# VectorE exps in fp16 with a set sign bit and a two-term polynomial, in a fused attention and GEGLU kernel

## Chip, cores, metric

One core of one Trainium2 chip. The metric is device time in microseconds (us), median of several executions.

## The reference

A pre-LayerNorm transformer block on 2048 tokens of width 512, 32 heads of width 16, in bf16:

```python
def _A_ref(x, wqkv, wo):          # attention
    ...
    scores = jnp.einsum("bhqd,bhkd->bhqk", q, k) * (Dh ** -0.5)
    p = _softmax(scores, axis=-1)
    o = jnp.einsum("bhqk,bhkd->bhqd", p, v)
    ...
def _B_ref(x, w_gate, w_up, w_down):
    return (_gelu(x @ w_gate) * (x @ w_up)) @ w_down
h  = x + _A_ref(_layernorm(x), A_wqkv, A_wo)
h2 = h + _B_ref(_layernorm(h), B_w_gate, B_w_up, B_w_down)
```

The work that matters is the softmax: 32 x 2048 x 2048 exponentials, in 2048 tiles of 128x512.

## The kernel before

The kernel has two complete paths. The fast path computes the softmax without subtracting a maximum and ends with a check of its row sums. If the check fails, every engine waits for the fast path's end and then runs a second, safe path (the `mx_` tiles) that subtracts the maximum.

```python
h.reg_load(r, flag[0:1, 0:1])
with h.If_ne(r, 128):              # 128 = every partition passed
    for sem, v in fin:
        if v:
            h.wait_ge(sem, v)
    FP.run(name, h)                # the second path
```

The reciprocals of the row sums are kept in `LINV`, with 16 columns for each of 40 units (a unit is a chunk of queries times a group of heads). Chunks are of 512, 512, 512, 256 and 256 queries; a unit of 256 queries writes only half of its columns:

```python
CHUNKS = (512, 512, 512, 256, 256)
LINV = at("LINV", [128, NUNIT, 16], FP32)
# [...] at the start, on GpSimd:
e.memset(LINV[:], 1.0)
# [...] at the end of unit u, nb = (queries of the chunk) / 128, so 4 or 2:
li = LINV[:, u, 0:4 * nb]...
e.reciprocal(out=li, in_=o4[:, :, :, 16])
# [...] the check, over the whole table; n = NUNIT * 16 = 640:
LCHK[:, n]   = (probe == 65535)                    # does the conversion to uint16 saturate?
LCHK[:, 0:n] = min(max(LINV, 2.0 ** -22), 2.0 ** 16) == LINV
lmin = reduce_min(LCHK)                            # then summed over 128 partitions into flag
```

(The last block is shortened from the four VectorE calls of the source.)

ScalarE does most exps, in steps of three and two tiles. VectorE does some, in groups of up to four tiles, from the bits of the score: `dX` is the score in units of 1/1024 octave (an octave is a factor of two of the exp) converted to uint16; the exponent bits become one factor, a polynomial of the mantissa the other. Matmuls, exps and VectorE's groups are put in order when the program is built, by a list scheduler that works with a modelled duration for every operation (the number after the engine's name). Each engine then runs its list in that fixed order.

```python
t1, t2 = 0.16 + 0.133 * n, 0.16 + 0.267 * n        # modelled us for n tiles
E = (X >> 3) & 0x1f80          # tensor_scalar, t1: 2^octave as bf16 bits
X = X & 0x3ff | 0x3c00         # tensor_scalar, t1: mantissa M as fp16 bits
W = M * M                      # tensor_tensor, t2
W = W * EK + EB                # tensor_scalar, t1
W = W * M                      # tensor_tensor, t2
T = W * E                      # tensor_tensor, t2
# P.V adds the products of V with E and with T
```

## Time and profile before

Before: 949.21 us, median of 3 (947.68 to 950.33). The parts that matter:

| what | before |
|---|---|
| span of the profiled run | 947.0 us |
| ScalarE (ACT) busy | 874.4 us, 92% |
| VectorE (DVE) busy | 735.3 us, 78% |
| exp tiles on ScalarE / on VectorE | 1832 / 216 |
| VectorE groups | 64 |

The busy line of the page of the kernel before (engine, busy us, share of the span, instructions; PE is TensorE's matmuls, PEld its weight loads, POOL is GpSimd):

```profile
PE 833.2 (88%) x7100; PEld 276.3 (29%) x7224; DVE 735.3 (78%) x1138; ACT 874.4 (92%) x817; POOL 220.5 (23%) x268
```

Groups of instructions of the kernel before, split by shape: line, engine, operation, output and input, count, then busy us and mean ns of one, then idle time just before them and what ended it. First the exps, then the three tensor-by-tensor products and the three operations with constants of one full VectorE group.

```profile
L1221 ACT ACTIVATE PT<-pbank 128x1536 bf16<-128x1536 f32 x366 | 555.3, 1517 | 21.1 <-PE pbank L1215 20.5
L1221 ACT ACTIVATE PT<-pbank 128x1024 bf16<-128x1024 f32 x367 | 402.1, 1096 | 3.7 <-PE pbank L1215 3.7
...
L1547 DVE TENSOR_TENSOR dX<-dW,dE_56 128x2048 bf16<-128x2048 f16 x42 | 54.7, 1303 | 0.6
L1545 DVE TENSOR_TENSOR dW<-dW,dX 128x2048 f16<-128x2048 f16 x42 | 52.4, 1248 | 1.0
L1543 DVE TENSOR_TENSOR dW<-dX 128x2048 f16<-128x2048 f16 x42 | 52.2, 1242 | 0.7
...
L1542 DVE TENSOR_SCALAR dX<-dX 128x2048 uint16<-128x2048 uint16 x42 | 31.0, 738 | 0.6
L1540 DVE TENSOR_SCALAR dE_56<-dX 128x2048 uint16<-128x2048 uint16 x42 | 30.6, 729 | 0.4
L1544 DVE TENSOR_SCALAR dW<-dW 128x2048 f16<-128x2048 f16 x42 | 29.7, 708 | 0.2
```

The idle column of the exps is the first thing to read: 24.8 us in all before 733 exps. ScalarE is the bound. Steps overlap at their ends: the two groups sum to 957.4 us, but the page's merged busy time of all exps is 841.0 us. So the cost of a tile is not 1517/3 ns but 841.0 us over 1832 tiles: 0.459 us.

Two stretches of 50 us of the kernel before, the first with attention alone, the second with an FFN block in flight (columns: stretch and its length, then busy us and instruction count of PE, PEld, DVE, ACT, POOL, then granted clock, DMA share, GB/s):

```profile
150.00:200.00 50.00, 43.25 (x341) 12.53 (x343) 46.29 (x61) 49.40 (x45) 0.00 (x0) 1.00 0.23 82
...
500.00:550.00 50.00, 43.78 (x304) 13.03 (x310) 43.40 (x60) 48.31 (x47) 25.05 (x21) 1.00 0.00 1
```

In attention alone VectorE is at 46 of 50 us and ScalarE at 49. In the FFN stretch GpSimd (POOL) runs three of the GELU's steps, and ScalarE is idle for 1.7 of 50 us, against 0.6 in the first stretch. Its waits in the whole kernel before (who waited for whom: us in total, times, longest us):

```profile
ACT PT L1221 <- PE pbank L1215: 24.2, 35, 2.8
ACT w_sb L1726 <- POOL w_sb L1719: 12.4, 15, 1.8
```

The second line: the Tanh of the GELU waiting for GpSimd. Three lines: the reciprocals and the check of the kernel before (the first two are groups by shape, the third is from the timeline, start and length first).

```profile
L1621 DVE RECIPROCAL LINV<-pbank 128x16 f32<-128x16 f32 x24 | 6.1, 252 | 11.2 <-PE pbank L1218 11.0
L1621 DVE RECIPROCAL LINV<-pbank 128x8 f32<-128x8 f32 x16 | 3.2, 200 | 4.8 <-PE pbank L1218 4.8
```

### The profile page before, as it was taken

How to read it: one execution, taken by the hardware profiler on the slowest of the kernel's cores; microseconds unless marked ns; L12 is line 12 of the kernel's file. 1: busy time of each engine (PE TensorE's matmuls, PEld its weight loads, DVE VectorE, ACT ScalarE, POOL GpSimd, SP SyncE). 2: the span in 40 equal slices, each digit the busy share in tenths (PEclk: the TensorE clock that was granted, in tenths of full speed). 3: DMA queues.
4: the chain of work that ended last, by engine and by line, in shares of the span. 5: the costliest groups of instructions: out<-in, count | busy, mean ns of one | idle time of the engine just before them, and what ended most of it. 6: DMA issues, size and time to landing. Idle time of an engine off the chain costs nothing.

```text
span 947.0 us, 17699 instructions
## 1 busy us (share of the span) xinstructions
PE 833.2 (88%) x7100; PEld 276.3 (29%) x7224; DVE 735.3 (78%) x1138; ACT 874.4 (92%) x817; POOL 220.5 (23%) x268
## 2 busy tenths in 40 slices
PE   8999888888898889888888988998898788899887
PEld 3322222222232222222222222222233222333345
DVE  7558989998979768699979788889958687643753
ACT  5789999999999999999999998999999799999962
POOL 6400000000027570000014564000003354302440
PEclk9999999999999999999999999999999899999999
DMA  5000006000000000000000000000000000000000
GB/s 178 1 1 1 1 1 244 1 2 1 12 2 1 1 1 12 23 1 2 1 12 1 1 1 1 12 23 1 1 8 19 1 1 1 2 12 24 2 7 21
DMA packets 12331, 15.13 MB, mean 16 GB/s; under 512 B 1744, under 2 KB 11216, under 8 KB 12240
## 3 DMA queue, kind: packets, MB, share of 16 engines
q1 hardware_dynamic: 12240, 13.90, 4.5%
q8 instruction: 59, 0.97, 0.5%
q14 instruction: 32, 0.26, 0.1%
HBM read 11.80 MB, written 2.10 MB: 15 GB/s over the span
## 4 chain that ended last, share of the span: by engine, by line
ACT 33%; PE 32%; DVE 16%; issue 14%; POOL 5%; ACTq 0%; DVEq 0%; POOLq 0%
ACT PT L1221 32%; PE pbank L1215 15%; PE pbank L1214 11%; PE pbank L1801 4%; POOL w_sb L1717 2%; DVE dX L1527 2%; POOL w_sb L1719 2%; DVE dW L1543 2%; DVE dE_56 L1540 1%; DVE dX L1542 1%; DVE dX L1547 1%; DVE g_sb L1715 1%; ACT w_sb L1726 1%; POOL w_sb L1718 1%; DVE w_sb L1727 1%
## 5 line engine op out<-in xcount | busy, mean ns | idle before, releaser
L1221 ACT ACTIVATE PT<-pbank 128x1536 bf16<-128x1536 f32 (+1 forms) x733 | 841.0, 1306 | 24.8 <-PE pbank L1215 24.2
L1215 PE MATMUL pbank<-QT,KT 32*128 32x512 bf16 (+1 forms) x2560 | 287.1, 341 | 71.7 <-ACT PT L1221 57.5
L1215 PE MATMUL pbank<-PT,VA 128*17 128x512 bf16 (+1 forms) x2307 | 187.6, 340 | 3.2 <-issue 1.8
L1527 DVE TENSOR_SCALAR dX<-pbank 128x512 uint16<-128x512 f32 x216 | 146.8, 686 | 45.9 <-PE pbank L1215 45.0
L1215 PEld LDWEIGHTS pbank<-QT,KT 32*128 32x128 bf16 x2560 | 77.0, 91 | 319.3 <-ACT PT L1221 220.6
L1801 PE MATMUL pbank<-ones_bf,zero_bf 128*128 128x512 bf16 x388 | 135.2, 388 | 13.5 <-DVE OA L1613 11.0
L1678 POOL TENSOR_SCALAR rstd_102<-mv_101 128x1 f32<-128x1 f32 x16 | 4.3, 269 | 510.4 <-DVE mv_101 L1676 510.3
L1717 POOL TENSOR_TENSOR w_sb<-g_sb 128x512 f32<-128x512 f32 (+1 forms) x56 | 65.3, 1166 | 168.2 <-DVE g_sb L1715 168.2
L1215 PEld LDWEIGHTS pbank<-PT,VA 128*17 128x17 bf16 x2307 | 47.5, 87 | 110.6 <-issue 98.1
L1547 DVE TENSOR_TENSOR dX<-dW,dE_56 128x2048 bf16<-128x2048 f16 (+3 forms) x64 | 73.2, 1144 | 1.0
L1719 POOL TENSOR_TENSOR w_sb<-w_sb,g_sb 128x512 f32<-128x512 f32 (+1 forms) x56 | 71.3, 1273 | 4.7
L1545 DVE TENSOR_TENSOR dW<-dW,dX 128x2048 f16<-128x2048 f16 (+3 forms) x64 | 71.0, 1109 | 1.4
L1543 DVE TENSOR_TENSOR dW<-dX 128x2048 f16<-128x2048 f16 (+3 forms) x64 | 70.7, 1105 | 1.2
L1801 PEld LDWEIGHTS pbank<-ones_bf,zero_bf 128*128 128x128 bf16 x459 | 37.3, 97 | 78.3 <-issue 61.7
L1727 DVE SCALAR_TENSOR_TENSOR w_sb<-w_sb,g_sb 128x512 f32<-128x512 f32 (+1 forms) x56 | 44.1, 787 | 20.6 <-ACT w_sb L1726 20.2
L1214 PE MATMUL pbank<-wd_sb,GUT 128*128 128x512 bf16 x211 | 56.0, 381 | 1.5 <-issue 1.3
L1715 DVE COPY g_sb<-pbank 128x512 f32<-128x512 f32 (+1 forms) x56 | 34.7, 619 | 18.6 <-PE pbank L1214 18.5
L1753 DVE SCALAR_TENSOR_TENSOR GUT<-pbank,w_sb 128x512 bf16<-128x512 f32 (+1 forms) x56 | 34.6, 619 | 15.5 <-PE pbank L1214 15.2
L1726 ACT ACTIVATE w_sb<-w_sb 128x512 f32<-128x512 f32 (+1 forms) x56 | 34.1, 609 | 12.4 <-POOL w_sb L1719 12.4
L1718 POOL TENSOR_SCALAR w_sb<-w_sb 128x512 f32<-128x512 f32 (+1 forms) x56 | 43.6, 779 | 4.9
L1540 DVE TENSOR_SCALAR dE_56<-dX 128x2048 uint16<-128x2048 uint16 (+3 forms) x64 | 43.5, 680 | 0.6
L1542 DVE TENSOR_SCALAR dX<-dX 128x2048 uint16<-128x2048 uint16 (+3 forms) x64 | 42.9, 670 | 1.2
(126 smaller groups left out, 694.0 us busy)
## 6 DMA issues: line engine op xcount, KB each, us to landing
xres<-in_A_x_dram SPq DMA_DIRECT2D x16, 128.0 KB, 2.2
out_dram<-out_sb SPq DMA_DIRECT2D x16, 128.0 KB, 1.7
wg_sb<-in_B_w_gate_dram SPq DMA_DIRECT2D x1, 1792.0 KB, 7.1
wu_sb<-in_B_w_up_dram SPq DMA_DIRECT2D x1, 1792.0 KB, 11.2
wd_sb<-in_B_w_down_dram SPq DMA_DIRECT2D x1, 1792.0 KB, 17.0
x_sb<-in_A_x_dram SPq DMA_DIRECT2D x3, 512.0 KB, 8.3
wqkv_sb<-in_A_wqkv_dram SPq DMA_DIRECT2D x1, 896.0 KB, 7.5
x_sb<-in_A_x_dram SPq DMA_DIRECT2D x2, 256.0 KB, 2.9
```

Of the source, the lines that this page charges most:

```text
L1214: return lambda e: e.matmul(o, l, r, start=start, stop=stop)
L1215: return lambda e: e.matmul(o, l, r, start=start, stop=stop, tile_position=tile)
L1221: return lambda e: e.activation(out=o, in_=i, func=func, **kw)
L1527: yield Op("dve", 0.7, lambda e: e.tensor_scalar(out=dX[:, G["k"] % NX, j, :], in0=pbank[:, b, :], scalar1=1024.0 * CENTER, scalar2=0.0, o ...
L1543: yield Op("dve", t2, lambda e: e.tensor_tensor(out=W, in0=M, in1=M, op=ALU.mult), reads=kX, writes=kW)
L1545: yield Op("dve", t2, lambda e: e.tensor_tensor(out=W, in0=W, in1=M, op=ALU.mult), reads=kW + kX, writes=kW)
L1547: yield Op("dve", t2, lambda e: e.tensor_tensor(out=T, in0=W, in1=E, op=ALU.mult), reads=kW + kE, writes=kX)
L1717: yield Op("pool", 0.1 + 1.03 * nq / 512, lambda e: e.tensor_tensor(out=ws, in0=gs, in1=gs, op=ALU.mult), reads=[("g", i)], writes=[("w", i)])
L1718: yield Op("pool", 0.1 + 0.7 * nq / 512, lambda e: e.tensor_scalar(out=ws, in0=ws, scalar1=GA, scalar2=1.0, op0=ALU.mult, op1=ALU.add), re ...
L1719: yield Op("pool", 0.1 + 1.2 * nq / 512, lambda e: e.tensor_tensor(out=ws, in0=ws, in1=gs, op=ALU.mult), reads=[("w", i), ("g", i)], write ...
L1727: yield Op("dve", 0.1 + 0.7 * nq / 512, lambda e: e.scalar_tensor_tensor(out=ws, in0=ws, scalar=1.0, in1=gs, op0=ALU.add, op1=ALU.mult), r ...
L1801: fill_op = Op("pe", TMM, lambda e: e.matmul(pbank[:, PVB, :], zero_bf[:], ones_bf[:], start=False, stop=False, skip_group_check=True), re ...
```

## The change

The intent is to drop one of the three products of a group. The score is converted with 32768 added, so its bits, read as fp16, are a negative number -2^e (1+m). That number is itself the last factor of the polynomial, and its exponent bits alone are the first term, so the separate product with M goes. The polynomial loses a term (1 + M (1 + EK M^2)). fp16 has fewer octaves than the bf16 layout, so the centre, the scales and the limits of the check move too. The core of the diff, cuts marked:

```diff
-CENTER = 40
-EC, EB, EK = 0.45805388, 1.01669147, 0.16656247
-VSCALE = 2.0 ** (127 - CENTER)
+XMIN = 32768.0
+CENTER = 12
+EC, EK = 0.46167356, 0.16665046
[...]
-    dE2 = at("dE2", [128, NE, GS, 512], BF16)
+    dE2 = at("dE2", [128, NE, GS, 512], F16)
[...]  V and its column of ones: VSCALE dropped; probe: floor 0 becomes XMIN; exp bias follows CENTER
-  dX = max(score + 1024.0 * CENTER, 0.0)
+  dX = max(score + XMIN + 1024.0 * CENTER, XMIN)
[...]
-  E = X >> 3 & 0x1f80 ; X = X & 0x3ff | 0x3c00 ; W = M * M ; W = W * EK + EB ; W = W * M ; T = W * E
+  W = X & 0x3ff | 0x3c00 ; W = W * W ; W = W * -EK - 1.0 ; E = X & 0x7c00 ; L = W * L
[...]
-  LCHK[:, 0:n] = min(max(lf, 2.0 ** -22), 2.0 ** 16)
+  LCHK[:, 0:n] = min(max(lf, 2.0 ** -16), 2.0 ** -7)
```

(The lines with dX, E to L and LCHK are shortened from the calls.)

More of the change, by code (lines that the diff above doesn't have):

```diff
@@ L1252, in consts @@
         yield Op("pool", 0.3, lambda e: e.tensor_copy(out=ident32[:], in_=ident[:]), reads=["ident"], writes=["ident32"])
-        yield Op("pool", 2.3, lambda e: e.memset(VA[:, :, :, 16:17], VSCALE), writes=["VA_ones"])
+        yield Op("pool", 2.3, lambda e: e.memset(VA[:, :, :, 16:17], 1.0), writes=["VA_ones"])
     def masks():
@@ L1261, in masks @@
         yield Op("dve", 0.5, lambda e: e.memset(pbank[:, PVB, :], 0.0), writes=[("pb", PVB)])
-        yield Op("dve", 0.1, lambda e: e.tensor_scalar(out=probe[:, 0:1], in0=ident32[:, 0:1], scalar1=1e6, scalar2=0.0, op0=ALU.add, op1=ALU.max), reads=["ident32"], writes=["probe"])
+        yield Op("dve", 0.1, lambda e: e.tensor_scalar(out=probe[:, 0:1], in0=ident32[:, 0:1], scalar1=1e6, scalar2=XMIN, op0=ALU.add, op1=ALU.max), reads=["ident32"], writes=["probe"])
     def ln1(c):
@@ L1370, in proj_v @@
                                       for dc in (2 * hf, 2 * hf + 1)], reads=rd, writes=[("pb", b)])
-            op = Op("dve", 0.61, lambda e, b=b, t=t: e.tensor_scalar(out=VA[:, t, :, 0:16], in0=pbank[:, b, :].rearrange("p (h i) -> p h i", i=16), scalar1=VSCALE, scalar2=None, op0=ALU.mult),
+            op = Op("dve", 0.61, lambda e, b=b, t=t: e.tensor_copy(out=VA[:, t, :, 0:16], in_=pbank[:, b, :].rearrange("p (h i) -> p h i", i=16)),
                     reads=[("pb", b)], writes=[("V", t)])
@@ L1486, in exps @@
             p0, n = an % NRING, len(mine)
-            yield Op("act", 0.093 + 0.427 * n, ACTF(PT[:, p0:p0 + n, :], pbank[:, b0:b0 + n, :], ACT.Exp, scale=LN2 / 1024, bias=-LN2 * (127 - CENTER) - math.log(EC)),
+            yield Op("act", 0.093 + 0.427 * n, ACTF(PT[:, p0:p0 + n, :], pbank[:, b0:b0 + n, :], ACT.Exp, scale=LN2 / 1024, bias=-LN2 * (15 - CENTER) - math.log(EC)),
                      reads=[("pb", b0 + k) for k in range(n)], writes=[("PT", p0 + k) for k in range(n)],
@@ L1526, in dconv @@
     def dconv(G, j, b):
-        yield Op("dve", 0.7, lambda e: e.tensor_scalar(out=dX[:, G["k"] % NX, j, :], in0=pbank[:, b, :], scalar1=1024.0 * CENTER, scalar2=0.0, op0=ALU.add, op1=ALU.max),
+        yield Op("dve", 0.7, lambda e: e.tensor_scalar(out=dX[:, G["k"] % NX, j, :], in0=pbank[:, b, :], scalar1=XMIN + 1024.0 * CENTER, scalar2=XMIN, op0=ALU.add, op1=ALU.max),
                  reads=[("pb", b)], writes=[("dX", G["k"] % NX, j)], gate=lambda: C["gpv"] >= G["k"] - NX + 1)
@@ L1535, in dchain @@
         X, W, E = dX[:, x, 0:n, :], dW[:, 0:n, :], dE2[:, d, 0:n, :]
-        M, T = X.bitcast(F16), X.bitcast(BF16)
+        L = X.bitcast(F16)
         kX, kW, kE = [("dX", x, j) for j in range(n)], ["dW"], [("dE", d)]
@@ L1539, in dchain @@
         yield Wait(lambda: G["conv"] == n)
-        yield Op("dve", t1, lambda e: e.tensor_scalar(out=E.bitcast(U16), in0=X, scalar1=3, scalar2=0x1f80, op0=ALU.logical_shift_right, op1=ALU.bitwise_and), reads=kX, writes=kE,
+        yield Op("dve", t1, lambda e: e.tensor_scalar(out=W.bitcast(U16), in0=X, scalar1=0x3ff, scalar2=0x3c00, op0=ALU.bitwise_and, op1=ALU.bitwise_or), reads=kX, writes=kW)
+        yield Op("dve", t2, lambda e: e.tensor_tensor(out=W, in0=W, in1=W, op=ALU.mult), reads=kW, writes=kW)
+        yield Op("dve", t1, lambda e: e.tensor_scalar(out=W, in0=W, scalar1=-EK, scalar2=-1.0, op0=ALU.mult, op1=ALU.add), reads=kW, writes=kW)
+        yield Op("dve", t1, lambda e: e.tensor_scalar(out=E.bitcast(U16), in0=X, scalar1=0x7c00, scalar2=None, op0=ALU.bitwise_and), reads=kX, writes=kE,
                  gate=lambda: C["gpv"] >= G["k"] - NE + 1)
-        yield Op("dve", t1, lambda e: e.tensor_scalar(out=X, in0=X, scalar1=0x3ff, scalar2=0x3c00, op0=ALU.bitwise_and, op1=ALU.bitwise_or), reads=kX, writes=kX)
-        yield Op("dve", t2, lambda e: e.tensor_tensor(out=W, in0=M, in1=M, op=ALU.mult), reads=kX, writes=kW)
-        yield Op("dve", t1, lambda e: e.tensor_scalar(out=W, in0=W, scalar1=EK, scalar2=EB, op0=ALU.mult, op1=ALU.add), reads=kW, writes=kW)
-        yield Op("dve", t2, lambda e: e.tensor_tensor(out=W, in0=W, in1=M, op=ALU.mult), reads=kW + kX, writes=kW)
         C["gw"] += 1
-        yield Op("dve", t2, lambda e: e.tensor_tensor(out=T, in0=W, in1=E, op=ALU.mult), reads=kW + kE, writes=kX)
+        yield Op("dve", t2, lambda e: e.tensor_tensor(out=L, in0=W, in1=L, op=ALU.mult), reads=kW + kX, writes=kX)
         G["done"] = 1
@@ L1582, in pv @@
                         for j, i in enumerate(G["t"]):
-                            fns += prod(i, [dE2[:, d, j, :], dX[:, x, j, :].bitcast(BF16)])
+                            fns += prod(i, [dE2[:, d, j, :], dX[:, x, j, :].bitcast(F16)])
                         fns = [f for _, f in sorted(fns, key=lambda a: a[0])]
@@ L1785, in check @@
         yield Op("dve", 0.1, lambda e: e.tensor_scalar(out=LCHK[:, n:n + 1], in0=probe[:, 0:1], scalar1=65535.0, scalar2=None, op0=ALU.is_equal), reads=["probe"] + [("LINV", u) for u in range(NU)], writes=["probe", "LCHK"])
-        yield Op("dve", 0.4, lambda e: e.tensor_scalar(out=LCHK[:, 0:n], in0=lf, scalar1=2.0 ** -22, scalar2=2.0 ** 16, op0=ALU.max, op1=ALU.min),
+        yield Op("dve", 0.4, lambda e: e.tensor_scalar(out=LCHK[:, 0:n], in0=lf, scalar1=2.0 ** -16, scalar2=2.0 ** -7, op0=ALU.max, op1=ALU.min),
                  reads=[("LINV", u) for u in range(NU)], writes=["LCHK"])
```

## The prediction

> **What bounds the kernel now.** ScalarE. The busy table gives ACT 874 us of a 947 us span (92%), DVE 735 (78%), PE 833 (88%, 135 of it zero-operand filler matmuls). The table by stretches of 50 us shows ACT at 46 to 50 of each 50 us from 50 to 900 us, but for one of 44.5; most of its 73 us idle lies in the first 50 us (18) and after 900 us (27). In the waits view the exps wait for PE only 24 us in all and the Tanh for GpSimd 12. So the middle is a nearly gapless row of exps: 366 of three tiles and 367 of two, 1832 tiles of 128x512 in 841 us busy, 0.459 us a tile. VectorE takes another 216 tiles in 64 groups. Its slowness costs time only through how few tiles it takes off ScalarE.
>
> **What the change does.** Per group, six chain operations become five: three with constants (about 0.7 us at 128x2048, in the groups split by shape) stay three; three tensor-by-tensor products (1.24, 1.25, 1.30 us) become two. The Trainium skill ("VectorE: DVE Perf Modes", the perf-mode tier table) lists 693 ns for tensor_scalar and 1224 ns for tensor_tensor at 2048 bf16 elements; this trace agrees (about 687 and 1220 ns in attention-only stretches), for fp16 and uint16 too, so I expect the new format to cost the same. V's 16 evacuations become plain PSUM copies, still 0.69 us. The second-product matmuls read fp16 instead of bf16; I take the rate as unchanged, about 385 ns.
>
> The dropped product cost 71 us in all. The schedule is laid out when the program is built, and reuses only part of that. Comparing instruction orders: groups go from 64 to 69, VectorE tiles from 216 to 231, exps from 733 to 727 (1817 tiles); projections, FFN and GpSimd work are unchanged; fillers go from 462 to 449.
>
> VectorE: minus 71 us, plus 15 conversions of 0.69 (10 us), plus five chains of about 4.6 us (23 us): 38 us less, near 697 us busy. ScalarE: minus 15 tiles at 0.459 = 6.9 us, so 867 us busy.
>
> **On the critical path.** VectorE's saving is almost wholly off it. ScalarE's 15 tiles are on it: 7 us. A shorter VectorE queue may shorten matmuls' waits, but these reach the exps only through their 24 us of waits; I allow 1 us. Head and tail do not change.
>
> **Predicted:** 949 - 7 - 1 = 941 us, 0.8% faster; 80% range 934 to 948. Chances: faster by over 2% 0.05, within 2% 0.92, slower by over 2% 0.03.
>
> **What would show it.** Exp busy 834 us, still 0.459 us a tile; ACT share near 92%. DVE near 697 us, remaining products 1.22 to 1.3 us, constants 0.7 us (the single AND too). Second-product matmuls about 385 ns. Exp waits for PE 20 to 28 us. Wrong if those waits grow, if chain steps leave their fast modes, or if the span shrinks by much more than 15 tiles' worth: then ScalarE's gaps came from VectorE after all.
>
> **What would make it wrong.** The static schedule is reshuffled from the first group on. Collisions in the FFN stretches, where Tanh waits for GpSimd, and GpSimd and VectorE slow each other (constants take 1.0 us there instead of 0.69), could move several us either way. If the row-sum check failed, the fallback would run and the time would about double; my own evaluation of the inputs puts scores below 13.1 octaves and row sums between 2^9.2 and 2^13.3, inside the check's limits, so under 2%.

## More of the kernel before

```profile
922.72 0.49 DVE L1786 TENSOR_SCALAR LCHK<-LINV 128x640 f32<-128x640 f32 x1
```

Multiply the shapes: 24 x 16 + 16 x 8 = 512 columns are written, 640 are checked.

Shorter times go with a higher clock: of 11 runs of the kernel before, the fastest took 945.82 us at 0.998 and the slowest 950.95 us at 0.988.

## The result

The changed kernel took 2408.94 us, median of 4 (2408.58 to 2410.47), against 949.53 us before (median of 4), with a correct result; the ratio is 2.538 (95% interval 2.534 to 2.542). Here and below a ratio is the mean time of one kernel's fast runs over that of the other's of the same rounds, so it is not quite the ratio of the medians quoted. Executions over 1.5% slower than the fastest of the same kernel are left out of the means.

The page of the changed kernel: the span and its busy line, and the two costliest groups.

```profile
span 2408.5 us, 42193 instructions
## 1 busy us (share of the span) xinstructions
PE 1933.9 (80%) x15458; PEld 579.8 (24%) x15722; DVE 1992.8 (83%) x3273; ACT 2157.5 (90%) x3284; POOL 668.1 (28%) x857
...
L506 DVE TENSOR_REDUCE mx_PM<-pbank 128x1 f32<-128x512 f32 x2048 | 1257.6, 683 | 70.8 <-PE pbank L547 57.6
L557 ACT ACTIVATE mx_PT<-pbank 128x512 bf16<-128x512 f32 x2048 | 1118.0, 604 | 79.7 <-PE pbank L547 9.6
```

The `mx_` tiles belong to the second path: the instruction count went from 17,699 to 42,193 because both paths ran. No operation became slow. The timeline shows the check, the flag, and the start of the second path (start us, length us, engine, line, operation, and in brackets idle time before it):

```profile
902.06 0.49 DVE L1787 TENSOR_SCALAR LCHK<-LINV 128x640 f32<-128x640 f32 x1
902.59 0.82 DVE L1789 TENSOR_TENSOR LCHK<-LCHK,LINV 128x640 f32<-128x640 f32 x1
903.45 0.82 DVE L1790 TENSOR_REDUCE lmin<-LCHK 128x1 bf16<-128x641 f32 x1
...
922.09 0.13 DVE L1793 CAST flag<-pbank 1x1 int32<-1x1 f32 x1
```

```profile
927.99 0.69 DVE L1772 TENSOR_TENSOR out_sb<-pbank,h_c_73 128x512 bf16<-128x512 f32 x1 [2.33 <-PE pbank L1214]
928.71 0.33 SPq L1775 DMA_DIRECT2D out_dram<-out_sb  x1
930.49 1.49 SPq L273 DMA_DIRECT2D mx_x_sb<-in_A_x_dram  x3
930.54 0.52 POOL L278 MEMSET mx_ones_bf<- 128x512 bf16 x1 [29.76 <-DMA out_dram<-out_sb]
```

So the fast path itself was done at about 930 us and the second path took the other 1478 us. Two questions follow: which part of the check failed, and what the fast path alone is worth.

The same two stretches in the changed kernel's first path:

```profile
150.00:200.00 50.00, 42.45 (x351) 12.17 (x355) 45.76 (x65) 49.36 (x44) 0.00 (x0) 1.00 0.12 39
...
500.00:550.00 50.00, 45.87 (x315) 13.16 (x319) 39.34 (x57) 48.45 (x48) 28.34 (x26) 1.00 0.01 1
```

ScalarE is as full as before in both.

### The profile page after: what moved, and what is told of

Same layout as the page of the kernel before. It is cut to its first block, busy times and chain, and to the rows that moved or that the text cites. A ratio compares the mean times of both kernels' runs of the same rounds, so it can differ in the third digit from the quotient of the medians.

```text
span 2408.5 us, 42193 instructions
## 1 busy us (share of the span) xinstructions
PE 1933.9 (80%) x15458; PEld 579.8 (24%) x15722; DVE 1992.8 (83%) x3273; ACT 2157.5 (90%) x3284; POOL 668.1 (28%) x857
## 4 chain that ended last, share of the span: by engine, by line
ACT 36%; PE 22%; DVE 22%; issue 17%; POOL 2%; DMA 0%; SPq 0%; ACTq 0%; POOLq 0%; DVEq 0%
DVE mx_PM L506 19%; ACT mx_PT L557 17%; ACT PT L1221 15%; PE pbank L497 7%; PE pbank L1215 6%; PE pbank L1214 4%; PE pbank L1802 1%; PE pbank L547 1%; PE pbank L772 1%; ACT mx_OA L419 1%; PE pbank L729 1%; PE pbank L748 1%; PE pbank L441 1%; ACT mx_u_sb L419 0%; ACT w_sb L1727 0%
## 5 line engine op out<-in xcount | busy, mean ns | idle before, releaser
L506 DVE TENSOR_REDUCE mx_PM<-pbank 128x1 f32<-128x512 f32 x2048 | 1257.6, 683 | 70.8 <-PE pbank L547 57.6
L557 ACT ACTIVATE mx_PT<-pbank 128x512 bf16<-128x512 f32 x2048 | 1118.0, 604 | 79.7 <-PE pbank L547 9.6
L1221 ACT ACTIVATE PT<-pbank 128x1536 bf16<-128x1536 f32 x727 | 834.0, 1309 | 19.0 <-PE pbank L1215 18.3
L497 PE MATMUL pbank<-mx_KT,mx_QT 32*128 32x512 bf16 x2048 | 399.4, 384 | 315.7 <-DVE mx_PM L506 165.0
L547 PE MATMUL pbank<-mx_QT,mx_KT 32*128 32x512 bf16 x2048 | 398.0, 385 | 4.9 <-ACT mx_PT L557 4.4
L1215 PE MATMUL pbank<-QT,KT 32*128 32x512 bf16 (+1 forms) x2560 | 284.7, 340 | 61.8 <-ACT PT L1221 45.8
L497 PEld LDWEIGHTS pbank<-mx_KT,mx_QT 32*128 32x128 bf16 x2048 | 104.9, 91 | 781.9 <-DVE mx_PM L506 773.5
L788 PE MATMUL pbank<-mx_ones_bf,mx_ident 128*128 128x512 bf16 x756 | 239.7, 385 | 5.2 <-ACT mx_PT L557 3.5
L591 POOL TENSOR_TENSOR mx_LINV<-mx_OAT,mx_negone 128x16 f32<-128x16 f32 x32 | 93.2, 2913 | 331.5 <-ACT mx_OAT L419 331.5
L568 PE MATMUL pbank<-mx_PT,mx_VA 128*17 128x512 bf16 x2048 | 156.8, 383 | 0.0
L547 PEld LDWEIGHTS pbank<-mx_QT,mx_KT 32*128 32x128 bf16 x2048 | 96.0, 91 | 23.6 <-ACT mx_PT L557 23.0
```

The lines of the kernel that those rows point to most:

```text
L497: P.op("pe", lambda e, g=g, b=b: e.matmul(pbank[:, b, :], QT[32 * g:32 * g + 32, c, slot, 128 * qt:128 * qt + 128], KT[32 * g:32 * g + 32, ...
L506: P.op("dve", lambda e, b=b, qt=qt, kc=kc, g=g: e.tensor_reduce(out=PM[:, par, qt, kc, g:g + 1], in_=pbank[:, b, :], axis=AX.X, op=ALU.max ...
L547: P.op("pe", lambda e, g=g, b=b: e.matmul(pbank[:, b, :], KT[32 * g:32 * g + 32, slot, 128 * kt:128 * kt + 128], QT[32 * g:32 * g + 32, c, ...
L557: P.op("act", lambda e, b=b, pi=pi: e.activation(out=PT[:, pi, :], in_=pbank[:, b, :], func=ACT.Exp), reads=[("pb", b)], writes=[("PT", pi)])
L568: P.op("pe", lambda e, g=g, kt=kt, pi=pi, slot=slot: e.matmul(pbank[32 * g:32 * g + 17, PVB, :], VA[:, kt, 4 * slot + g, :], PT[:, pi, :], ...
L591: P.op("pool", lambda e: e.tensor_tensor(out=li, in0=oat4[:, :, :, 16], in1=negone[:].rearrange("p (q g) -> p q g", g=4), op=ALU.pow), rea ...
```

## The experiments

Theory A: the 640 - 512 = 128 columns of the table that no unit writes keep the fill of 1.0; it lay inside the old limits (up to 2^16) and lies outside the new ones (up to 2^-7). Rival B: real row sums left the new limits, or fp16 made an inf or a NaN. Rival C: the saturation probe, now with a floor of 32768, fails.

### Which entry of the check failed

**fill_in**, the changed kernel with one number changed, the limits left as narrow as they are:

```diff
-e.memset(LINV[:], 1.0)
+e.memset(LINV[:], 2.0 ** -10)
```

> The changed kernel with one number changed: the table of reciprocal row sums is first filled with 2^-10 instead of 1.0. Theory A (the entries of the table that no unit writes, 8 of 16 columns in the 16 units of 256 queries, keep the fill of 1.0 and fail the new upper limit of 2^-7): the check passes, no second path in the trace, correct result, 930 to 936 us, since the first path's last output left at 930.5 us in the changed kernel's trace. Rival B (real row sums outside the limits, or inf or NaN from fp16) and rival C (the saturation probe fails): the second path still runs, 2409 us.

Measured: correct, 934.49 us (934.10 to 934.77, 4 runs) against 948.30 us before (11 runs), ratio 0.9857 (0.9837 to 0.9877). Its page:

```profile
span 932.2 us, 17691 instructions
## 1 busy us (share of the span) xinstructions
PE 827.0 (89%) x7105; PEld 274.1 (29%) x7228; DVE 692.0 (74%) x1114; ACT 867.1 (93%) x811; POOL 210.3 (23%) x268
```

The two products that are left in a full group (of 128x2048), in the same run:

```profile
L1548 DVE TENSOR_TENSOR dX<-dW,dX 128x2048 f16<-128x2048 f16 x47 | 61.0, 1298 | 0.8
L1543 DVE TENSOR_TENSOR dW<-dW 128x2048 f16<-128x2048 f16 x47 | 59.3, 1262 | 0.8
```

The instruction count is back at one path. The real row sums and the probe passed the narrow check in this run, so B and C fall.

**fill_edge**: the fill is 2^-6, one octave over the limit. 

> The changed kernel with the table filled with 2^-6, just over the new upper limit of 2^-7. Theory A (unwritten entries decide): the second path runs, about 2409 us. If something other than the fill decides, the time equals that of the run with 2^-10.

Measured: 2407.78 us (one run), 42,193 instructions again.

**limit_one**: the fill stays 1.0 and only the upper limit is raised:

```diff
-scalar1=2.0 ** -16, scalar2=2.0 ** -7
+scalar1=2.0 ** -16, scalar2=1.0
```

> The changed kernel with its fill of 1.0 and only the check's upper limit raised from 2^-7 to 1.0. Theory A: passes, 930 to 936 us. Rivals (real sums too small in the other direction, NaN, probe): 2409 us.

Measured: 934.40 us (one run), span 932.5 us.

**before_fill_out**: the kernel before, with its own wide limits and bf16 chain, filled with 2^17. 

> The kernel before, with the table filled with 2^17, over its own upper limit of 2^16, and nothing else changed. Theory A: the second path runs here too, at 949 + about 1475 us = 2425 us, so the fill alone makes the 2.5-fold time without any fp16. Rival: the written entries cover the table, and the time stays 949 us.

Measured: 2424.01 us (one run) beside 950.21 us for the kernel before. The second path costs 2424.01 - 950.21 = 1473.8 us here, and 2408.94 - 934.49 = 1474.5 us with the change. The fill alone turns one path into two, in either arithmetic. Theory A is shown.

### What the fast path gained

With the check mended, the change is worth 948.30 - 934.49 = 13.8 us, where 8 had been predicted. That is less than 2%, but its interval (0.9837 to 0.9877) lies clear of 1. A kernel on this schedule changes in two ways at once: VectorE has less to do per group, and the scheduler lays out another order with 15 more tiles on VectorE. The next kernels separate them.

**frozen**: the mended kernel, but the scheduler is given the old chain's durations and dependences; the dropped product is replaced by a copy of one column. The order of matmuls, ScalarE and GpSimd work was compared with the kernel before and is identical.

```diff
-W = W * M                                       # before, modelled at t2
+dscr[:, 0:1] = ident32[:, 0:1]                  # one column, still modelled at t2
```

> As fill_in, but the scheduler is told the old chain (same modelled times and dependences, the dropped product replaced by a one-column copy), so that matmuls, exps and GpSimd work stand in exactly the order of the kernel before, with 216 VectorE tiles. Theory 'VectorE's saved time is off the critical path': 946 to 950 us, ratio 0.997 to 1.000. Rival 'a lighter VectorE itself shortens the waits of matmuls and exps': 936 to 943 us.

Measured: 941.41 us (6 runs), ratio 0.992 (0.990 to 0.994). The theory that VectorE's saving is off the critical path falls: without one tile fewer on ScalarE, 6.9 us are gone. The rival's time is met. ScalarE's busy time is that of before, so the gain is idle time:

```profile
span 940.1 us, 17699 instructions
...
PE 832.3 (89%) x7100; PEld 276.2 (29%) x7224; DVE 677.1 (72%) x1138; ACT 874.2 (93%) x817; POOL 212.3 (23%) x268
```

Its waits:

```profile
ACT PT L1222 <- PE pbank L1216: 24.1, 37, 2.8
...
ACT w_sb L1729 <- POOL w_sb L1722: 5.8, 11, 1.0
```

The exps wait as long as before (24.1 against 24.2 us), so the shorter waits of exps that the rival gives as its reason did not come; the Tanh waits for GpSimd 5.8 us instead of 12.4. That difference, 6.6 us, is nearly all of the gain and points to the FFN stretches. The test is to put the product back in one kind of stretch only.

**third_all, third_ffn, third_attn**: as frozen, with a harmless third product (`W = max(W, W)`, the same size and kind) in all 64 groups, in the 34 whose chain runs with an FFN block in flight, or in the other 30. Orders on PE, ScalarE and GpSimd are identical to the kernel before in all three.

```diff
-dscr[:, 0:1] = ident32[:, 0:1]
+W = max(W, W)    # where: all / FFN block in flight / otherwise; else the one-column copy
```

> As frozen (new arithmetic, order of the kernel before), with a third product put back in all 64 groups (max of the tile with itself, which changes no value). Control for the format: if fp16 in itself costs nothing, this is the kernel before again, ratio 0.998 to 1.002.

> As frozen, with the third product put back only in the 34 groups whose chain runs while an FFN block is in flight. Theory D (frozen gained its 7 us in the FFN stretches, where a shorter VectorE queue lets GpSimd's and ScalarE's GELU steps come sooner): ratio 0.998 to 1.000, as before. Theory E (it gained in the attention-only stretches, where VectorE is 90% busy): stays at 0.991 to 0.993. Evenly spread: 0.996.

> As frozen, with the third product put back only in the other 30 groups, in the attention-only stretches. Theory D: stays at 0.991 to 0.993. Theory E: 0.998 to 1.000. Evenly spread: 0.996.

Measured on one chip, with the kernel before at 949.04 us (11 runs):

| kernel | third product in | median us | ratio to before, 95% | Tanh's wait for GpSimd |
|---|---|---|---|---|
| third_all | 64 groups | 948.14 | 0.9995 (0.997 to 1.002) | 12.4 us |
| third_ffn | 34, FFN in flight | 949.64 | 1.001 (0.998 to 1.004) | 12.5 us |
| third_attn | 30, attention alone | 941.28 | 0.9915 (0.989 to 0.994) | 5.9 us |
| frozen (other chip) | none | 941.41 | 0.992 (0.990 to 0.994) | 5.8 us |

All of the gain comes from the FFN stretches and none from attention alone, although VectorE is fuller there and the products put back are about as much work (36.4 us busy in third_ffn, 34.6 in third_attn). The start times of ScalarE's instructions, which stand in the same order in both traces, show the same: third_attn is level with the kernel before at 250 us, ahead by 2.2 us at 350 and still at 500, by 4.5 at 600 and still at 700, and by 7.0 at 800. It gains only while FFN blocks are in flight. third_all also clears the format: fp16 with the new centre and a third product costs what the kernel before costs. The product makes GpSimd slower as well. The last GELU step on GpSimd, first in third_ffn, then in third_attn (groups by shape):

```profile
L1727 POOL TENSOR_TENSOR w_sb<-w_sb,g_sb 128x512 f32<-128x512 f32 x42 | 60.9, 1450 | 3.5
```

```profile
L1727 POOL TENSOR_TENSOR w_sb<-w_sb,g_sb 128x512 f32<-128x512 f32 x42 | 57.2, 1362 | 3.5
```

The Trainium skill ("SBUF — State Buffer", section "SBUF: two separate sides") says that a VectorE operation with two SBUF inputs and a GpSimd operation that reads SBUF exclude each other on a shared pair of ports. The trace agrees in direction: with the product the mean is 1450 ns, without it 1362. GpSimd's busy time in all is 220.8 us in third_ffn and 212.8 in third_attn. How much of the Tanh's wait comes from this and how much from VectorE's longer queue (it also does the GELU's first copy) was not separated.

The rest, 941.41 - 934.49 = 6.9 us, goes with the new order and its 15 tiles. ScalarE's busy time falls from 874.2 us (frozen) to 867.1 us (fill_in), by 7.1 us; 15 x 0.459 is 6.9. ScalarE's idle time hardly differs, 65.9 us in frozen and 65.1 in fill_in, but its waits are others. In fill_in:

```profile
ACT PT L1221 <- PE pbank L1215: 19.5, 28, 2.8
...
ACT w_sb L1727 <- POOL w_sb L1720: 9.8, 15, 2.4
```

The Tanh waits 9.8 us here, not 5.8, and the exps 19.5, not 24.1. So the two halves add up in time, but the first is not the same wait in the new order.

**tuned**: as fill_in, the scheduler's limit on VectorE's queue raised from 0.8 to 1.4 us; 237 VectorE tiles instead of 231.

> As fill_in, but the scheduler may open a group when VectorE's queue is up to 1.4 us ahead instead of 0.8: 237 VectorE tiles instead of 231, exps 725 instead of 727. Theory 'each tile moved is worth 0.46 us of ScalarE': 2 to 4 us under fill_in. Rival 'the order decides more than the count': anywhere within 6 us of fill_in on either side.

Measured: 938.77 us (4 runs), ratio 0.989 (0.987 to 0.992): 4.3 us slower than fill_in with six tiles fewer on ScalarE. ScalarE's busy time hardly fell further in its profile (866.5 against 867.1 us), while the exps waited longer for matmuls:

```profile
ACT PT L1221 <- PE pbank L1215: 28.4, 37, 2.8
```

The profiled run is the slowest of the four, 941.59 us at a clock of 0.989 (fill_in: 0.995), so part of the 4.3 us may be the clock; but the fastest, 936.54 us at 0.994, is still above all four runs of fill_in (934.10 to 934.77, at 0.993 to 0.995). The idea of a fixed price per tile falls: six tiles should have saved 2.8 us, and no run was faster. The order counts too.

**fewer_in_ffn**: as fill_in, with the scheduler holding back groups while an FFN block is in flight (`DBUSY` 2 to 10); 224 VectorE tiles.

> As fill_in, but the scheduler waits 10 us longer, instead of 2, before it opens a group while an FFN block is in flight: 224 VectorE tiles and 730 exps instead of 231 and 727. Theory 'a tile is worth 0.46 us of ScalarE and nothing else': 3 us slower than fill_in's 0.986, near 0.989. Theory 'VectorE's load in the FFN stretches costs as well': at or under 0.986.

Measured: 940.92 us (6 runs), ratio 0.992 (0.989 to 0.995). The second theory is not borne out: the Tanh's wait was 4.9 us against fill_in's 9.8, yet the whole is about 6 us slower than fill_in (by the ratios, as it ran on another chip), more than the 3 us that seven tiles would explain. Again the exps waited longer for matmuls, 25.0 us. What in the order does it was not found.

**extra, extra_attn**: exactly the order of fill_in, but with a useless third product per group that the scheduler does not know of; in all 69 groups, or only in 34 of them, in attention-only stretches.

```diff
+E = L * L                 # fp16, then a semaphore wait, then the real E:
 E = X & 0x7c00
```

> As fill_in with exactly its instruction order, but with a third useless product of 16-bit tiles per group that the scheduler does not know of (about 80 us more of VectorE). Theory 'the gain is the 15 tiles taken off ScalarE and the new order': within 3 us of fill_in. Rival 'the gain comes from VectorE having less to do': back to 942 us or more.

> As extra (fill_in's order, a third product unknown to the scheduler), but only in the 34 of 69 groups whose chain runs in attention-only stretches. extra lost 58 us. Saturation of VectorE in the attention-only stretches (46 of 50 us busy, plus about 6 us for 5 products): 955 us or more. If the loss belongs to the FFN stretches, as in the order of the kernel before: 934 to 940 us.

Measured: extra 992.41 us (6 runs), ratio 1.047 (1.043 to 1.050); extra_attn 962.46 us (4 runs), ratio 1.014 (1.012 to 1.017). My expectation for extra, within 3 us of fill_in, missed by 55 us; the rival, 942 us or more, is the one that was met. About half of the loss comes from the 34 groups in attention alone, where VectorE went from 45.8 to 48.7 of 50 us in both kernels. The stretch from 150 to 200 us, first in fill_in, then in extra:

```profile
150.00:200.00 50.00, 42.29 (x349) 12.06 (x352) 45.76 (x65) 49.36 (x45) 0.00 (x0) 1.00 0.12 36
```

```profile
150.00:200.00 50.00, 40.47 (x311) 11.24 (x315) 48.69 (x66) 46.54 (x41) 0.00 (x0) 0.97 0.25 88
```

VectorE has become the bound there and ScalarE idles. A rival is the granted clock, which was lower as well: 0.963 in the profiled run of extra and 0.979 in extra_attn, against 0.995. The same stretch of extra_attn had the full clock (1.00), and ScalarE is still down to 47.2 us, from 49.4, so the loss does not need a lower clock:

```profile
150.00:200.00 50.00, 39.91 (x321) 11.42 (x326) 48.75 (x66) 47.18 (x42) 0.00 (x0) 1.00 0.24 83
```

What the clock adds to the whole loss was not separated. The chain that ended last points to VectorE too, in shares of the span, first fill_in, then extra:

```profile
ACT 40%; PE 29%; issue 17%; DVE 8%; POOL 3%; DMA 1%; SPq 0%; ACTq 0%; DVEq 0%
```

```profile
DVE 44%; PE 29%; ACT 16%; issue 8%; POOL 1%; DMA 1%; SPq 0%; ACTq 0%; DVEq 0%
```

Put beside third_attn, this is the lesson of the pair: a product in attention-only groups costs nothing in an order laid out with that product in it, and about 0.8 us a group (27 us over 34 groups, from the ratio 1.014 over 0.9857 times 934.5 us) in an order laid out without it. The load explains it as well as the order does: fill_in's order has filled the saved time with more groups, so that VectorE is at 45.8 of 50 us without the product and at 48.7 with it, while third_attn with its product is at 46.3. The two differ also in the place of the product in the chain and in one semaphore wait, so this compares the whole, not the order alone.

fill_in is the fastest version found and beats both kernels.

## Why the prediction was wrong

- **The step that failed** is the path: that the check passes and only the first path runs. It stands in the last paragraph, "my own evaluation of the inputs puts scores below 13.1 octaves and row sums between 2^9.2 and 2^13.3, inside the check's limits, so under 2%". The sums were right: with another fill the real entries and the probe pass (fill_in). What was wrong is the belief that the check reads only row sums. It reads 640 columns, 512 are written, and the other 128 hold the fill of 1.0, which the new limit of 2^-7 excludes. So the second path ran every time: 934.49 + 1474.5 us instead of 941. The cost of that case was mis-sized too: "about double" measured 2.54 times. The profile of before showed the numbers (128x16 x24, 128x8 x16, 128x640), and the diff showed the new limits; neither was multiplied out.
- **What bounds the kernel**: ScalarE, right. fill_in's ScalarE is busy 93% of the span.
- **Work removed and added**: right. VectorE near 697 us busy, measured 692.0 in fill_in and 691.7 in the first path of the changed kernel (up to 930.4 us); ScalarE 867 predicted, 867.1 measured; exps 834 predicted, 833.6 measured; second-product matmuls about 385 ns, measured 384 to 389. The exps' waits for PE, foreseen at 20 to 28 us, were 19.5.
- **"VectorE's saving is almost wholly off it ... I allow 1 us"**: a mis-sized term. It measured 6.9 us (frozen), all in the FFN stretches (third_ffn against third_attn) and in the Tanh's waits, not in the exps' waits that the sum looked at. The prediction's own warning, a span that shrinks by much more than 15 tiles' worth, came true: 13.8 us against 7. I had named those stretches as a risk and not as part of the sum.
- **"ScalarE's 15 tiles are on it: 7 us"**: consistent with the 6.9 us between frozen and fill_in and with ScalarE's busy time. That each tile has this price in any order is refuted by tuned.
- The mended kernel, at 934.49 us, lies at the low end of the stated range of 934 to 948, but that was a statement about a kernel that was not the one on record.

## What to carry to other kernels

When a kernel guards a fast path, treat its guard as part of the change: list every entry that the check reads, including padding and entries that only the initial fill has written, and test each against the new limits. When one engine's work is cut under a fixed instruction order, rebuild the kernel with the old order to see what the cut is worth alone; here the cut alone was worth 6.9 us, nearly all in a neighbour's waits, and the new order with its 15 tiles another 6.9. VectorE time in the stretches where GpSimd works was on the critical path here, though VectorE was less full there (43 of 50 us) than in attention alone (46).

## What the Trainium skill lacked or had wrong

- "VectorE: DVE Perf Modes", the perf-mode tier table, has times for bf16 and fp32 only (what the page says of the modes themselves speaks of 16-bit types in general). These runs add times for fp16 and uint16 at 128x2048: in attention-only stretches about 1220 ns for fp16 products and 683 to 690 ns for bitwise and multiply-add operations with constants, close to the bf16 column's 1224 and 693. Over the whole kernel before, FFN stretches included, the means were 1242 to 1303 and 708 to 738 ns.
- "SBUF — State Buffer" says that the shared ports are held for a whole instruction but gives no size for a mixed stream. Here 34 more VectorE products, 36.4 us in all, in the FFN stretches instead of 30 in attention alone moved GpSimd's last GELU step from 1362 to 1450 ns on average, with 8 us between the two kernels (949.64 against 941.28).
- "TensorE: Matmul & The Clock Gate" gives no rate for an fp16 moving tile against bf16 weights. In fill_in such matmuls of 512 columns took 384 to 389 ns by the profile's model, and those with bf16 on both sides 385.
